# Transposing DMAs singly behind k loads, expert weights behind the last y store, last logits from 16-bit parts

## The chip, the cores and the metric

The kernel runs on one core of a Trainium2 chip. Its engines work in parallel, each through its own queue of instructions: TensorE (PE, with the loading of weights shown as PEld), VectorE (DVE), ScalarE (ACT), GpSimd (POOL) and SyncE (SP), which here does little but issue DMAs, one after the other in the order of its queue. An engine that waits for a semaphore holds everything behind it in its queue. The metric is the device time of one execution in microseconds, the median of several runs.

## The reference

Three stages, each fed by the one before, all in float32:

```python
scores = scale * np.matmul(q, k.transpose(0, 1, 3, 2))       # 4 x 8 heads x 576 x 64
scores = np.where(mask, scores + bias[None], -1000000000.0)  # window of 128, ALiBi
attn = softmax(scores);  x = np.matmul(attn, v)              # -> (2304, 512)

h = x @ w_in                                                 # 512 -> 2048
g = np.maximum(h, 0.0) + alpha * np.minimum(h, 0.0)
y = g @ w_out                                                # 2048 -> 512

logits = y @ w_gate                                          # 512 -> 8
order = np.argsort(-logits.flatten())                        # greedy: best logits first,
...                                                          # one expert a token, 288 tokens an expert
out[mask] = np.maximum(y[mask] @ w1[e], 0.0) @ w2[e]         # for each of 8 experts
```

## The kernel before, in words

Up to about 551 us, attention and the MLP are interleaved. The MLP goes in 9 units `u` of 256 tokens (`NU = 9`), each in 16 slices `f` of 128 hidden columns (`FT = 16`); one slice of one unit is a slot, 144 in all. Attention is done in blocks of 128 tokens and halves of 4 heads, some slots ahead of the unit that needs it. What is done in which slot is written in a table: `at(slot, fn, args)` puts a step at a slot, and the loop goes through the slots. A scheduler with a simulated timeline then sets the order on each engine; within one engine it may put a step earlier or later than the table has it, and `tc.issue_after(instruction)` keeps what is issued in its block behind the named instruction.

For a slice, `l1` (L697) makes the first layer: 12 matmuls of 128x256 into the bank `ph` (products of two fp16 parts each). ACT scales it to `g` (L703), DVE takes the leaky maximum (L704), ACT rounds to fp16 `gh` (L722) and DVE takes the rest `gl` (L723). `l2` (L740) makes the second layer: 6 matmuls of 128x512 into `py`. In the last unit those of the last 11 slices (`ND = 11`) aren't done at once but kept in the list `rest`, to fill PE during the first search of the routing; `gh` and `gl` then lie in tiles `gs`.

The logits of the last unit don't wait for its y. `og` (L854, slots 125.5 to 128.5) multiplies a transposed copy of w_out with w_gate into the combined weights `WG` (float32), and `last_logits` (L670) adds, for every slice, two float32 matmuls of `g` with `WG` into `PL`, from which `last_y` makes the logits. The transposed copies, `wt`, are made by `og_load`: 8 transposing DMAs (L846) for each of 4 groups, all 8 at one place of the table, the groups at slots 60, 68, 76, 84 (`OG0 = 60`, `OGS = 8`). They are issued from SP's queue, as are the loads of q (L386), k (L406), v (L412) and the stores of y (L768). A v load needs the one buffer `vr`, whose last reader is DVE's L498; its first reader is L451.

Behind the last unit comes the routing, expert by expert: a search for the threshold, in five passes (PE matmuls and DVE operations, with `fill` taking second-layer matmuls from `rest` between them), then `index`, then `gather` (L1215: POOL's indirect DMAs read the expert's rows of y back from `y_dram`). In the first round `last_rows` scales the last two blocks of y on ACT (L1208) and stores them (L1209). `warm` (L1036) are matmuls without use that fill PE. `expert_weights` loads 512 KB for each of 8 slices of an expert (L1226, three buffers `wr`), ACT rounds them (L1231) and POOL or DVE takes the rest (L1234). `expert_x` transposes the gathered rows (L1267), `expert_1` (L1283), `expert_2` (L1301) and `expert_y` make the expert's output, which POOL scatters to `out`.

Of the kernel before, what the change touches and what calls it, by code (L numbers as in the profile page):

```python
# [8 lines left out]
F32 = mybir.dt.float32  # L9
F32R = mybir.dt.float32r  # L10
F16 = mybir.dt.float16
BF16 = mybir.dt.bfloat16
# [4 lines left out]
ALU = mybir.AluOpType  # L17
AX = mybir.AxisListType

LABEL = None  # L20
P = 128
H = 8
# [4 lines left out]
LEAST = 896 * 16  # L27
KG = 15
FW = 20
ND, OG0, OGS, OG1 = 11, 60, 8, 125.5  # L30
FILL = (6, 4, 12, 5, 5, 5, 2, 11, 99)
FG_ = 1
WP, WX_ = 10, 3
# [71 lines left out]
def attention_moe_kernel(ctx, tc, qt, kt, vt, wm, alpha, wg, we, out, NB=18, dbg=None):  # L105
    nc = tc.nc
    NU = NB // 2
# [3 lines left out]
    FT = 16  # L111
# [13 lines left out]
    wh, wl = {}, {}  # L125
# [228 lines left out]
        return "plain"  # L354


    QR, QH, QL, KR, VP, E, SM, ET, S_, XN = ({} for _ in range(10))
    XF, XH, XL, MN, VG, VI, VC, XS = {}, {}, {}, {}, {}, {}, {}, {}
    XT_ = {}
# [42 lines left out]
    def load_k(n):  # L402
        b, hf = divmod(n, 2)
        KR[n] = att.tile([P, 4, P], F32, name="kr", bufs=KB)
        for i in range(2):
            nc.sync.dma_start(KR[n][i * 64:(i + 1) * 64], kt[b, hf])  # L406

    def load_v(n):
        b, hf = divmod(n, 2)
# [250 lines left out]


    GF, GH, GL, PY, PH, GS = {}, {}, {}, {}, [], {}
    PL, rest, LAST = [], [], {}

    def last_logits(f):
        g = GF.pop((NU - 1, f))
        if not f:
            PL.append(psum.tile([P, 2, H], F32, name="pl", tag="sA", bufs=1))
        for i in range(2):
            LAST["pl"] = nc.tensor.matmul(PL[0][:, i], g[:, i * P:(i + 1) * P], WG[:, f], start=f + i == 0, stop=f == FT - 1,  # L670
                             skip_group_check=True)

    def prefill():
        rest.sort(key=lambda e: e[:3])
# [51 lines left out]
    def l2(u, f):  # L726
        if f == 0:
            PY[u] = [psum.tile([P, 512], F32, name=f"py{i}", tag=f"py{i}") for i in range(2)]
        if u < EARLY_U:
            g = GF.pop((u, f))  # L730
            for i in range(2):
                nc.tensor.matmul(PY[u][i], g[:, i * P:(i + 1) * P], wf[f][:, 512:], start=f == 0, stop=f == FT - 1)  # L732
            return
        gh, g = GH.pop((u, f)), GL.pop((u, f))
        if u == NU - 1:
            last_logits(f)
        for i in range(2):
            for j, (a, w) in enumerate(((gh, wh), (gh, wl), (g, wh))):
                def one(i=i, j=j, a=a, w=w):
                    nc.tensor.matmul(PY[u][i], a[:, i * P:(i + 1) * P], w[f][:, 512:], start=f == 0 and j == 0,  # L740
                                     stop=f == FT - 1 and j == 2)
                if u < NU - 1 or f < FT - ND:
                    one()
                else:
                    rest.append((i, f, j, one))
        if u == NU - 1 and f == FT - 1:
            rest.sort(key=lambda e: e[:3])
            rest[:] = [e[3] for e in rest]
# [74 lines left out]
    def last_y():  # L823
        u = NU - 1
        fill(FILL[1])
        nc.vector.tensor_scalar(L[:, NB - 2:], PL[0], YI[:, u:u + 1], None, op0=ALU.mult)
        find_scale()
        R[0]["cmp"] = best_of(R[0], slice(NB - 2, NB))

# [2 lines left out]
    def thirds(dst, src, rest):  # L832

        nc.scalar.activation(dst[0], src, AF.Copy)
        nc.vector.tensor_sub(rest, src, dst[0])
        nc.scalar.activation(dst[1], rest, AF.Copy)
        nc.vector.tensor_sub(dst[2], rest, dst[1])

    WG = consts.tile([P, FT, H], F32, name="wog")
    WT = {}  # L840

    def og_load(j):
        WT[j] = wpool.tile([P, 4, 2, 4, P], F16, name="wt", tag=f"wd{4 + j}")
        for i in range(4):
            for k, w in enumerate((wh, wl)):
                nc.sync.dma_start_transpose(out=WT[j][:, i, k], in_=w[4 * j + i][:, 512:])  # L846

    def og(j):
        t = WT.pop(j)
        pl = psum.tile([P, 4, 3, H], F32, name="pl", tag="pav" if j % 2 else "sB", bufs=1)  # L850
        for i in range(4):
            for c in range(4):
                for k in range(2):
                    nc.tensor.matmul(pl[:, i], t[:, i, k, c], wg3[:, c], start=c + k == 0, stop=c + k == 4)  # L854
        nc.vector.tensor_reduce(WG[:, 4 * j:4 * j + 4], pl.rearrange("p f i e -> p f e i"), axis=AX.X, op=ALU.add)

    def gate_parts():
        r = mlp.tile([P, 4, H], F32, name="wgr", tag="yt", bufs=1)
# [45 lines left out]
    def at(s, fn, *a):  # L904
        ev.setdefault(math.floor(s), []).append((s, len(ev.get(math.floor(s), ())), fn, a))
# [57 lines left out]
        at(WC + f, w_split, f)  # L963
    at(WC - .5, w_scales)
    for j in range(4):
        at(OG0 + OGS * j, og_load, j)
        at(OG1 + j, og, j)

    def do(fn, *a):
# [234 lines left out]
    def last_rows():  # L1204
        for i in range(2):
            b, u = NB - 2 + i, NU - 1
            y = ex.tile([P, 512], F32, name="row", bufs=3)
            LAST["row"] = nc.scalar.activation(y, PY[u][i], AF.Copy, scale=YI[:, u:u + 1])  # L1208
            nc.sync.dma_start(y_dram[b * P:(b + 1) * P], y)  # L1209

    def gather(p):
        r = R[p]
# [7 lines left out]
    def expert_weights(p, f):  # L1220
# [2 lines left out]
            r["reg"] = nc.sync.value_load(r["ei"][0:1, 0:1], min_val=0, max_val=NE - 1)  # L1223
        s = (p % 2) * 8 + f
        w = ex.tile([P, 1024], F32, name="wr", bufs=3)
        nc.sync.dma_start(w, we[bass.ds(r["reg"], 1), f].rearrange("o p n -> (o p) n"))  # L1226
        w_slot(s)
        for i in range(2):
            h = slice(i * 512, (i + 1) * 512)
# [272 lines left out]
```

## Time and profile before

| what | before |
|---|---|
| median of 3 runs | 849.34 us (848.4 to 850.53) |
| profiled execution | 849.54 us |
| its span | 847.8 us |
| mean granted TensorE clock | 0.965 |
| PE busy | 801.5 us (95%) |
| PEld busy | 652.2 us (77%) |
| DVE busy | 577.8 us (68%) |
| ACT busy | 457.9 us (54%) |
| POOL busy | 278.9 us (33%) |
| first-layer matmuls (L697) | 1536, 199.3 us |

The busy times overlap, so they don't add up to the span. The span is what the profiler's records cover; the execution's own time is 1.7 us longer. Shares of the whole span say little on a kernel in stages; the rows further down are of single stretches. A name like L846 is a line of the kernel before.

### The profile page before, as it was taken

How to read it: one execution, taken by the hardware profiler on the slowest of the kernel's cores; microseconds unless marked ns; L12 is line 12 of the kernel's file. 1: busy time of each engine (PE TensorE's matmuls, PEld its weight loads, DVE VectorE, ACT ScalarE, POOL GpSimd, SP SyncE). 2: the span in 40 equal slices, each digit the busy share in tenths (PEclk: the TensorE clock that was granted, in tenths of full speed). 3: DMA queues.
4: the chain of work that ended last, by engine and by line, in shares of the span. 5: the costliest groups of instructions: out<-in, count | busy, mean ns of one | idle time of the engine just before them, and what ended most of it. 6: DMA issues, size and time to landing. Idle time of an engine off the chain costs nothing.

```text
span 847.8 us, 18203 instructions
## 1 busy us (share of the span) xinstructions
PE 801.5 (95%) x6854; PEld 652.2 (77%) x6854; DVE 577.8 (68%) x1748; ACT 457.9 (54%) x1097; POOL 278.9 (33%) x256
## 2 busy tenths in 40 slices
PE   7789999979999999999999999997999989999996
PEld 5667676757777767777777777856999879999995
DVE  6897688958687687887868753685677766752120
ACT  4899367746555565655655543413465444455531
POOL 4244020001110010101100000008799976888921
PEclk7699999999999999999999999997999999999998
DMA  8997101654021031121201000025466655556500
GB/s 298 278 350 235 33 26 50 119 106 138 26 84 51 30 98 41 47 80 51 81 33 38 2 2 26 2 99 152 148 199 194 197 163 170 156 175 198 165 29 29
DMA packets 49144, 93.22 MB, mean 110 GB/s; under 512 B 22800, under 2 KB 22816, under 8 KB 49056
## 3 DMA queue, kind: packets, MB, share of 16 engines
q1 hardware_dynamic: 45984, 82.62, 32.4%
q0 software_dynamic: 3072, 9.44, 3.5%
q8 instruction: 54, 0.88, 0.4%
q14 instruction: 34, 0.28, 0.1%
HBM read 78.40 MB, written 9.44 MB: 104 GB/s over the span
## 4 chain that ended last, share of the span: by engine, by line
PE 77%; DVE 9%; ACT 4%; DMA 3%; issue 3%; SPq 2%; POOL 2%; another core or an unknown queue 0%; POOLq 0%; ACTq 0%; DVEq 0%
PE ph L697 21%; PE py L740 17%; PE pyx L1301 12%; PE phx L1283 10%; PE S L533 3%; PE py L732 2%; SPq L846 2%; PE pav L627 2%; PE pav L619 2%; PE prt L1072 2%; PE pt L568 1%; DVE wf L182 1%; DMA vr<-in_v_dram 1%; DMA wr<-in_we_dram 1%; PE pt L648 1%
## 5 line engine op out<-in xcount | busy, mean ns | idle before, releaser
L697 PE MATMUL ph<-xh,wp 128*128 128x256 f16 x1536 | 199.3, 273 | 0.3 <-DVE g L704 0.3
L697 PEld LDWEIGHTS <-wp 128*128 128x128 f16 x1536 | 148.6, 99 | 42.3 <-issue 1.6
L1234 POOL TENSOR_TENSOR ws<-wr,ws 128x512 fp32r<-128x512 f32 x128 | 160.2, 1286 | 13.4 <-ACT ws L1231 12.4
L434 POOL TENSOR_TENSOR ks<-kr,ks 64x512 fp32r<-64x512 f32 x34 | 49.0, 1447 | 289.0 <-ACT ks L433 277.8
L740 PE MATMUL py<-wp,gh 128*128 128x512 f16 x468 | 131.3, 381 | 4.8 <-ACT gh L722 4.8
L703 ACT ACTIVATE g<-ph,sg 128x256 f32<-128x256 f32 x144 | 67.3, 468 | 101.5 <-PE ph L697 100.1
L1301 PE MATMUL pyx<-hh,ws 128*128 128x288 f32 x512 | 109.6, 300 | 0.0
L1231 ACT ACTIVATE ws<-wr 128x512 fp32r<-128x512 f32 x128 | 73.4, 627 | 50.6 <-DMA wr<-in_we_dram 35.8
L704 DVE SCALAR_TENSOR_TENSOR g<-ph,sa,g 128x256 f32<-128x256 f32 x144 | 69.1, 480 | 44.3 <-ACT g L703 44.0
L1283 PE MATMUL phx<-exh,ws 128*128 128x288 f32 x512 | 86.8, 307 | 0.2
L1301 PEld LDWEIGHTS pyx<-hh,ws 128*128 128x128 f32 x512 | 84.4, 188 | 0.0
L740 PE MATMUL py<-wp,gl 128*128 128x512 f16 x234 | 78.7, 382 | 0.6 <-DVE gl L723 0.6
L1283 PEld LDWEIGHTS phx<-exh,ws 128*128 128x128 f32 x512 | 74.9, 194 | 1.0 <-PE pox L1319 0.4
L1301 PE MATMUL pyx<-hl,ws 128*128 128x288 f32 x256 | 75.5, 295 | 0.0
L722 ACT ACTIVATE gh<-g 128x256 f16<-128x256 f32 x117 | 48.4, 413 | 49.3 <-DVE g L704 43.4
L740 PEld LDWEIGHTS <-gh 128*128 128x128 f16 x468 | 44.0, 98 | 36.1 <-ACT gh L722 5.4
L723 DVE TENSOR_TENSOR gl<-g,gh 128x256 f16<-128x256 f32 x117 | 53.1, 454 | 16.1 <-ACT gh L722 15.9
L1290 DVE SCALAR_TENSOR_TENSOR hl<-phx,hh 128x288 fp32r<-128x288 f32 x64 | 28.7, 454 | 51.7 <-ACT hh L1289 50.8
L559 ACT ACTIVATE e<-e,mn 128x128 f32<-128x128 f32 x116 | 45.1, 391 | 10.6 <-DVE mn L556 10.4
L1289 ACT ACTIVATE hh<-phx 128x288 fp32r<-128x288 f32 x64 | 25.4, 405 | 43.6 <-PE phx L1283 31.4
L1301 PEld LDWEIGHTS pyx<-hl,ws 128*128 128x128 f32 x256 | 48.2, 188 | 0.0
L1283 PE MATMUL phx<-exl,ws 128*128 128x288 f32 x256 | 46.9, 307 | 0.0
(291 smaller groups left out, 1549.9 us busy)
## 6 DMA issues: line engine op xcount, KB each, us to landing
wr<-in_we_dram SPq DMA_DIRECT2D x64, 512.0 KB
raw<-in_wm_dram SPq DMA_DIRECT2D x16, 1023.8 KB
kr<-in_k_dram SPq DMA_DIRECT2D x68, 128.0 KB
qr<-in_q_dram SPq DMA_DIRECT2D x64, 128.0 KB
y_dram<-y SPq DMA_DIRECT2D x16, 256.0 KB
vr<-in_v_dram SPq DMA_DIRECT2D x13, 256.0 KB
whole<-in_v_dram SPq DMA_DIRECT2D x4, 256.0 KB
whole<-in_q_dram SPq DMA_DIRECT2D x4, 128.0 KB
```

The costliest lines, as they stand in the source:

```text
L434: nc.gpsimd.tensor_sub(ks[64:], KR[n][64:], f32(ks[64:]))
L559: nc.scalar.activation(e[:, h], e[:, h], AF.Exp, bias=mn[:, h:h + 1], scale=-1.0, accum_out=SM[b][:, hh:hh + 1])
L697: LAST["l1"] = nc.tensor.matmul(ph, w[f][:, c * P:(c + 1) * P], x[u][:, c, :], start=i == 0, stop=i == 4 * len(pairs) - 1)
L703: KEPT[order.index((u, f))] = nc.scalar.activation(g, ph, AF.Copy, scale=sg)
L704: TURN[order.index((u, f))] = nc.vector.scalar_tensor_tensor(g, ph, sa, g, op0=ALU.mult, op1=ALU.max)
L722: nc.scalar.activation(gh, g, AF.Copy)
L723: nc.vector.tensor_sub(gl, g, gh)
L740: nc.tensor.matmul(PY[u][i], a[:, i * P:(i + 1) * P], w[f][:, 512:], start=f == 0 and j == 0, stop=f == FT - 1 and j == 2)
L1231: nc.scalar.activation(wh[s][:, h], w[:, h], AF.Copy)
L1234: (nc.vector if on_dve else nc.gpsimd).tensor_sub(wl[s][:, h], w[:, h], f32(wh[s][:, h]))
L1283: nc.tensor.matmul(ph, w[s][:, c * P:(c + 1) * P], x[:, c], start=i == 0, stop=i == 11)
L1301: nc.tensor.matmul(py, w[s][:, cs], r[x][f], start=i == 0, stop=i == 23)
```

## The change

Three parts. The first: the 32 transposing DMAs of w_out stand singly in the table, every second slot from 48 on (48, 50, ... 110), each kept behind the k load that was issued last. The second: of expert 0's weight loads only the first (`WE = 1`) may go ahead of the store of the last y rows; the others are kept behind it. The third: the last unit's logits of slices 0 to 14 are made of the parts `gh` and `gl` and of `WG` split in three bf16 parts (`WG3`; `gh` with three of them, 24 columns, `gl` with two, 16 columns), into four columns of partial sums that one DVE reduction adds; slice 15 stays in float32. The split of `WG` is 4 small operations for each of 4 groups, two on ACT and two on DVE.

```diff
-ND, OG0, OGS, OG1 = 11, 60, 8, 125.5
+ND, OG0, OGS, OG1 = 11, 48, 2, 125.5
+WE = 1
...
-            nc.sync.dma_start(KR[n][i * 64:(i + 1) * 64], kt[b, hf])
+            LAST["ld"] = nc.sync.dma_start(KR[n][i * 64:(i + 1) * 64], kt[b, hf])
...
     def last_logits(f):
         g = GF.pop((NU - 1, f))
         if not f:
-            PL.append(psum.tile([P, 2, H], F32, name="pl", tag="sA", bufs=1))
+            PL.append(psum.tile([P, 2, 4, H], F32, name="pl", tag="sA", bufs=1))
         for i in range(2):
-            LAST["pl"] = nc.tensor.matmul(PL[0][:, i], g[:, i * P:(i + 1) * P], WG[:, f], start=f + i == 0, stop=f == FT - 1,
-                             skip_group_check=True)
+            s = slice(i * P, (i + 1) * P)
+            if f == FT - 1:
+                LAST["pl"] = nc.tensor.matmul(PL[0][:, i, 3], g[:, s], WG[:, f], start=False, stop=True,
+                                              skip_group_check=True)
+                continue
+            for j, (a, k) in enumerate(((GH, 3), (GL, 2))):
+                nc.tensor.matmul(PL[0][:, i, :k], a[NU - 1, f][:, s], WG3[:, f, :k], start=f + i + j == 0,
+                                 stop=f == FT - 2, skip_group_check=True)
...
-        nc.vector.tensor_scalar(L[:, NB - 2:], PL[0], YI[:, u:u + 1], None, op0=ALU.mult)
+        new = L[:, NB - 2:]
+        nc.vector.tensor_reduce(new, PL[0].rearrange("p b i e -> p b e i"), axis=AX.X, op=ALU.add)
+        nc.vector.tensor_scalar(new, new, YI[:, u:u + 1], None, op0=ALU.mult)
...
-    def og_load(j):
-        WT[j] = wpool.tile([P, 4, 2, 4, P], F16, name="wt", tag=f"wd{4 + j}")
-        for i in range(4):
-            for k, w in enumerate((wh, wl)):
-                nc.sync.dma_start_transpose(out=WT[j][:, i, k], in_=w[4 * j + i][:, 512:])
+    def og_load(m):
+        j, i, k = m // 8, m % 8 // 2, m % 2
+        if m % 8 == 0:
+            WT[j] = wpool.tile([P, 4, 2, 4, P], F16, name="wt", tag=f"wd{4 + j}")
+        with tc.issue_after(LAST["ld"].ins):
+            nc.sync.dma_start_transpose(out=WT[j][:, i, k], in_=(wh, wl)[k][4 * j + i][:, 512:])
...
-        nc.vector.tensor_reduce(WG[:, 4 * j:4 * j + 4], pl.rearrange("p f i e -> p f e i"), axis=AX.X, op=ALU.add)
+        wj = WG[:, 4 * j:4 * j + 4]
+        nc.vector.tensor_reduce(wj, pl.rearrange("p f i e -> p f e i"), axis=AX.X, op=ALU.add)
+        r = mlp.tile([P, 4, H], F32, name="wgr", tag="yt", bufs=1)
+        thirds([WG3[:, 4 * j:4 * j + 4, i] for i in range(3)], wj, r)
...
-        at(OG0 + OGS * j, og_load, j)
+        for m in range(8 * j, 8 * j + 8):
+            at(OG0 + OGS * m, og_load, m)
...
-            nc.sync.dma_start(y_dram[b * P:(b + 1) * P], y)
+            LAST["store"] = nc.sync.dma_start(y_dram[b * P:(b + 1) * P], y)
...
-        nc.sync.dma_start(w, we[bass.ds(r["reg"], 1), f].rearrange("o p n -> (o p) n"))
+        with nullcontext() if p or f < WE else tc.issue_after(LAST["store"].ins):
+            nc.sync.dma_start(w, we[bass.ds(r["reg"], 1), f].rearrange("o p n -> (o p) n"))
```

In what follows, `wp_...` are the fp16 parts of the MLP's weights, `vr`, `kr`, `qr` the buffers of v, k and q. First SP's queue, in the middle of the interleaved stage. Before:

```order
L846 DMA_TRANSPOSE wt<-wp_1250 128x4x128 x4
L406 DMA kr<-in_k_dram 64x512 x2
L386 DMA qr<-in_q_dram 64x512 x2
L846 DMA_TRANSPOSE wt<-wp_1367 128x4x128 x4
L846 DMA_TRANSPOSE wt<-wp_1474 128x4x128 x4
L846 DMA_TRANSPOSE wt<-wp_1580 128x4x128 x4
L412 DMA vr<-in_v_dram 128x512
L846 DMA_TRANSPOSE wt<-wp_1695 128x4x128 x4
```

SP's queue now, from the place of the first transposes:

```order
L408 DMA kr<-in_k_dram 64x512 x2
L858 DMA_TRANSPOSE wt<-wp_1097 128x4x128 x2
L388 DMA qr<-in_q_dram 64x512 x2
L408 DMA kr<-in_k_dram 64x512 x2
L858 DMA_TRANSPOSE wt<-wp_1097 128x4x128 x2
L408 DMA kr<-in_k_dram 64x512 x2
L858 DMA_TRANSPOSE wt<-wp_1172 128x4x128 x2
L414 DMA vr<-in_v_dram 128x512
```

The transposes stood in blocks, twelve of them in a row ahead of one v load; they stand in ones and twos, behind k loads, and eleven of the 32 directly ahead of a v load (five times two, once one). The first stands several k, q and v loads later than before.

PE in the last unit, at the end of one slice's first layer and the start of the next's. Before (`wog` is `WG`):

```order
L697 LDWEIGHTS wp_1474
L697 MATMUL ph<-xh,wp_1474 128x256
L670 MATMUL pl<-wog,g 128x8 x2
L697 LDWEIGHTS wp_1580
L697 MATMUL ph<-xh,wp_1580 128x256
```

PE at such a place now (`wog_164` is `WG3`, `gs` holds `gh` and `gl`):

```order
L705 LDWEIGHTS wp_1581
L705 MATMUL ph<-xh,wp_1581 128x256
L678 LDWEIGHTS gs
L678 MATMUL pl<-wog_164,gs 128x24
L678 LDWEIGHTS gs
L678 MATMUL pl<-wog_164,gs 128x16
L678 LDWEIGHTS gs
L678 MATMUL pl<-wog_164,gs 128x24
L678 LDWEIGHTS gs
L678 MATMUL pl<-wog_164,gs 128x16
L705 LDWEIGHTS wp_1581
```

One float32 group of two became four 16-bit matmuls with their weight loads; they work on the slice two slots back.

SP's queue around the two stores of the last y rows (L1209 before, L1225 now). Before:

```order
L768 DMA y_dram<-y 128x512 x4
L1209 DMA y_dram<-row 128x512
L1223 TENSOR_LOAD ei
L1223 ISA x2
L1226 ISA
L1226 DMA wr<-in_we_dram 128x1024
L1226 ISA
L1226 DMA wr<-in_we_dram 128x1024
L1226 ISA
L1226 DMA wr<-in_we_dram 128x1024
L1209 DMA y_dram<-row 128x512
```

The same place now:

```order
L776 DMA y_dram<-y 128x512 x4
L1225 DMA y_dram<-row 128x512
L1239 TENSOR_LOAD ei
L1239 ISA x2
L1243 ISA
L1243 DMA wr<-in_we_dram 128x1024
L1225 DMA y_dram<-row 128x512
L1243 ISA
L1243 DMA wr<-in_we_dram 128x1024
```

Three loads of expert weights stood ahead of the second store; now it is one.

## Rows read from the trace of the kernel before

**Rows 1.** Page, chain of work that ended last: shares of the span by engine

```profile
PE 77%; DVE 9%; ACT 4%; DMA 3%; issue 3%; SPq 2%; POOL 2%; another core or an unknown queue 0%; POOLq 0%; ACTq 0%; DVEq 0%
```

**Rows 2.** Windows: us, busy (count) of PE PEld DVE ACT POOL, PEclk, DMA share, GB/s

```profile
180.00:200.00 20.00, 15.53 (x118) 11.40 (x116) 11.84 (x39) 9.81 (x28) 2.54 (x2) 0.83 0.58 145
200.00:548.00 348.00, 344.27 (x3160) 258.42 (x3159) 258.24 (x762) 190.56 (x509) 27.97 (x22) 1.00 0.15 46
```

**Rows 3.** Timeline of SP's queue: start us, us, queue, line, operation, out<-in, count

```profile
167.41 16.62 SPq L846 DMA_TRANSPOSE wt<-wp  x12
184.13 0.53 SPq L412 DMA_DIRECT2D vr<-in_v_dram  x1
```

**Rows 4.** Timeline of DVE and PE, 177 to 191 us: [idle before <-releaser]

```profile
177.64 0.75 DVE L498 SCALAR_TENSOR_TENSOR v<-vr,vc,v 128x512 f16<-128x512 f32 x1 [0.79 <-ACT v L493]
...
187.09 0.69 DVE L451 TENSOR_REDUCE vc<-vr 128x1 f32<-128x512 f32 x1 [6.25 <-DMA vr<-in_v_dram]
...
188.67 1.89 PE L740 MATMUL py<-wp,gh 128*128 128x512 f16 x4 [4.47 <-ACT gh L722]
```

**Rows 5.** Windows of 1 us, columns as in rows 2 (PEclk third from the right)

```profile
187.00:188.00 1.00, 0.00 (x0) 0.00 (x0) 0.91 (x2) 0.00 (x0) 0.00 (x0) 0.71 0.73 142
...
194.00:195.00 1.00, 1.00 (x10) 0.91 (x9) 0.98 (x3) 0.00 (x0) 0.00 (x0) 0.88 0.88 332
```

**Rows 6.** Chain that ended last, in order of time: start us, us, what

```profile
184.13 2.94 DMA vr<-in_v_dram
...
238.92 2.78 DMA vr<-in_v_dram
```

**Rows 7.** Waits of DVE and of SP's queue, whole span: us in sum, count, longest

```profile
DVE vc L451 <- DMA vr<-in_v_dram: 14.2, 9, 6.3
...
SPq L412 <- DVE v L498: 26.1, 4, 15.9
```

**Rows 8.** Chain that ended last, one slice of the last unit

```profile
538.48 0.35 PE pl L670 x4
538.82 1.32 PE ph L697 x12
```

**Rows 9.** Timeline of PE: the matmuls on transposed w_out

```profile
513.32 0.95 PE L854 MATMUL pl<-wg,wt 128*128 128x24 bf16 x32
```

**Rows 10.** Timeline of DVE and ACT in the last unit

```profile
529.61 0.18 DVE L877 TENSOR_REDUCE L<-pl 128x8 f32<-128x24 f32 x1 [1.44 <-PE pl L876]
...
548.61 0.47 ACT L703 ACTIVATE g<-ph,sg 128x256 f32<-128x256 f32 x1 [0.23 <-PE ph L697]
...
549.64 0.42 ACT L722 ACTIVATE gs<-g 128x256 f16<-128x256 f32 x1 [0.55 <-DVE g L704]
```

**Rows 11.** Timeline of SP's queue, 556 to 570 us

```profile
559.02 0.32 SPq L1209 DMA_DIRECT2D y_dram<-row  x1
565.56 1.43 SPq L1226 DMA_DIRECT2D wr<-in_we_dram  x3
568.65 0.34 SPq L1209 DMA_DIRECT2D y_dram<-row  x1
```

**Rows 12.** Timeline of ACT, POOL and PE, 572 to 583 us

```profile
572.74 1.15 ACT L1231 ACTIVATE ws<-wr 128x512 fp32r<-128x512 f32 x2 [0.58 <-DMA wr<-in_we_dram]
...
574.33 1.13 POOL L1215 DMA_INDIRECT xg<-y_dram,ix  x1 [19.81 <-DVE rs L1061]
...
581.71 0.90 PE L1267 MATMUL ptx<-ident,xg 96*128 96x96 f32 x4 [1.18 <-DMA xg<-y_dram,ix]
```

**Rows 13.** Windows around the stores and the gather, columns as in rows 2

```profile
560.50:561.00 0.50, 0.50 (x16) 0.28 (x12) 0.47 (x4) 0.00 (x0) 0.00 (x0) 1.00 0.08 25
...
572.00:573.00 1.00, 1.00 (x11) 0.90 (x10) 0.90 (x3) 0.42 (x2) 0.00 (x0) 1.00 0.11 43
...
586.00:587.00 1.00, 1.00 (x22) 1.00 (x22) 0.41 (x3) 0.81 (x2) 1.00 (x2) 0.61 0.84 98
```

**Rows 14.** Waits of ACT, expert phase: us in sum, count, longest

```profile
ACT hh L1289 <- remote: 3.9, 1, 3.9
```

More of the change, by code (lines that the diff above doesn't have):

```diff
@@ L354, in kind_of @@
         return "plain"
+    LAST = {}
     QR, QH, QL, KR, VP, E, SM, ET, S_, XN = ({} for _ in range(10))
@@ L662, in attention_moe_kernel @@
     GF, GH, GL, PY, PH, GS = {}, {}, {}, {}, [], {}
-    PL, rest, LAST = [], [], {}
+    PL, rest = [], []
     def last_logits(f):
@@ L733, in l2 @@
             return
-        gh, g = GH.pop((u, f)), GL.pop((u, f))
         if u == NU - 1:
             last_logits(f)
+        gh, g = GH.pop((u, f)), GL.pop((u, f))
         for i in range(2):
@@ L839, in attention_moe_kernel @@
     WG = consts.tile([P, FT, H], F32, name="wog")
+    WG3 = consts.tile([P, FT, 3, H], BF16, name="wog3")
     WT = {}
-    def og_load(j):
-        WT[j] = wpool.tile([P, 4, 2, 4, P], F16, name="wt", tag=f"wd{4 + j}")
-        for i in range(4):
-            for k, w in enumerate((wh, wl)):
-                nc.sync.dma_start_transpose(out=WT[j][:, i, k], in_=w[4 * j + i][:, 512:])
+    def og_load(m):
[4 more added lines that the diff above has]
+            nc.sync.dma_start_transpose(out=WT[j][:, i, k], in_=(wh, wl)[k][4 * j + i][:, 512:])
     def og(j):
```

## The prediction

> **What bounds the kernel now.** I began with the chain of work that ended last, summed by engine: TensorE (PE) holds 77% of it, SP's queue only 2% and DMA 3% [rows 1]. So time can be won only where PE stops, or does work that can be done in less; and a stop is to be judged in its own stretch. The table by stretch says where that is: from 200 to 548 us PE is busy 344.27 of 348 us at a granted clock of 1.00, but from 180 to 200 only 15.53 of 20, at a mean clock of 0.83 [rows 2]. The rest of the reading is of three places.
>
> The first place is that stretch. SP works through twelve transposing DMAs from 167.41 on, 16.62 us long, 1.39 each, and only then, at 184.13, issues the load of the next v block [rows 3]. Its buffer was free at 178.39: that is when VectorE's (DVE) last read of the old block ends, 177.64 + 0.75 [rows 4]. The load lands 2.94 us after its issue [rows 6], DVE starts on it at 187.09 after waiting 6.25 us, and PE, which needs what DVE makes of it, resumes at 188.67 after 4.47 us of idleness [rows 4]. The granted clock falls in 187 to 188 (mean 0.71: the fall from 2.4 to 1.2 GHz lies at 187.4) and is back in 194 to 195 (mean 0.88: at 194.24) [rows 5]. So PE was idle to 188.67 and then ran 5.57 us at the half clock.
>
> The second is the last unit of tokens, where PE alternates between twelve matmuls of the first layer, 1.32 us, and one float32 group of logits, 0.35 us [rows 8].
>
> The third is the end of the search, where GpSimd (POOL) gathers the rows of expert 0 at 574.33. SP issues three loads of expert weights from 565.56 and the store of the last y rows only at 568.65 [rows 11].
>
> **The transposes, spread (A).** Nothing is computed less: 32 of them stay, and their data moves at a DMA share of 0.15 [rows 2], so it is a matter of SP's queue alone. Removed: the block of twelve ahead of the v load. It would be issued at about 178.5 and land at 181.4, 5.7 us sooner. PE's work after it, 188.67 before, could begin at 183.0; but PE had other work until 188.67 − 4.47 = 184.20, so all of the 4.47 goes, and no more. With the gap goes, if the gap is what the clock fell on, the stretch at half clock: 5.57 us in which half of the work is done, so 2.8 us. What is late next there is DVE: it is busy 11.84 of the 20 us [rows 2], and without the wait of 6.25 the same work has 13.75 us, which leaves it 86% full; PE may be held by it in small pieces.
>
> Added: in the new order a transpose or two stands directly ahead of six of the later v loads, eleven in all, and others behind k loads, ahead of q loads and y stores. A v load that is ready goes at most 2 × 1.39 us later. SP has slack for it: in four waits, 26.1 us in sum, it stands idle for a v buffer [rows 7], and time spent on a transpose before the buffer is free costs nothing. On the other side, DVE waited for v data nine times, 14.2 us in sum, 6.3 of it the case above [rows 7]; the other eight share 7.9, so v data comes just in time. I find one load with no slack and take half a transpose for it, 0.7; from 0 to 1.39 for the one, and the rival below for all. The queue behind, q, k and y, has whole slots of slack. A = 4.47 + 2.8 − 0.7 = 6.6; bounds 7.3 (no cost) and 3.8 (the clock falls all the same).
>
> **The logits in parts (C).** For each of the first fifteen slices a group of 0.35 us [rows 8] is replaced by four small matmuls on 16-bit parts, 24 and 16 columns wide. The nearest row is the kernel's own 128x24 bf16 matmul on transposed weights: 32 of them in 0.95 us, 0.030 each, and so 0.12 us for four [rows 9]. PE saves 0.23 a slice. In the first five slices, where second-layer matmuls fill in, that is 5 × 0.23 = 1.15. In the next ten ScalarE (ACT) comes in: its g starts at 548.61, it waits 0.55 for DVE, and its gh ends at 549.64 + 0.42 = 550.06, 1.45 us in all [rows 10]; PE would need 1.32 + 0.12 = 1.44, before 1.67. With a little for the hand-over a slice goes from 1.67 to 1.46: 10 × 0.21 = 2.1. Against it stands one reduction more on DVE in the tail, 0.18 by its like [rows 10], on the way to the search: 0.2. The sixteen small operations that split the gate weights, eight on DVE at 0.18 each, 1.4 us, lie in a region where DVE is busy 258.24 of 348 us [rows 2]; I put them at nothing, and at 1.4 if that cover is gone. C = 1.15 + 2.1 − 0.2 = 3.1. The upper bound is 15 × 0.23 − 0.2 = 3.3. The lower one is below nothing: if each small matmul with its weight load costs what one of the twelve does, 1.32 / 12 = 0.11, then a slice takes 0.44, 0.09 more than now, and C = −15 × 0.09 − 0.2 = −1.6. I take the upper side because the 32 differ from these only in a few columns.
>
> The row shows 30 ns for a small matmul with its weight load. The Trainium skill, "TensorE: Matmul & The Clock Gate", section "Back-to-back issue gap", gives about 81 ns for a sustained pair of weight load and matmul of 128 columns; by that figure a slice would cost 0.32, C would be 0.2 and the time 840.8. The trace disagrees for narrow ones, by [rows 9].
>
> **The store ahead of two loads (B).** Before, the second store of y rows goes out behind three loads of 512 KB and its data lies in the queues with theirs: the DMA engines fall to a share of 0.11 only in 572 to 573 [rows 13]. POOL's gather starts at 574.33, 2.2 us after the data's end at about 572.1, though the profile names a DVE operation as what ended the wait [rows 12]. The first store, alone in its queue, was issued at 559.02 and in 560.5 to 561 the engines are all but empty, a share of 0.08 [rows 11, 13]: so 1.6 us. With one load only ahead, the second store is done at about 568.65 + 1.6 = 570.25 and the gather can start at 572.4: 1.9 us sooner. What then moves along: POOL's weight differences, and PE's first transposes of gathered rows, which wait for the gather [rows 12]. The two loads behind the store go 3.4 us later and land near 574; their last ACT conversion, at 572.74 before [rows 12], would end near 575.5, well ahead of PE's first use at 582, so it is hidden; without that cover it would cost what they are late, 1.6. B = 1.9. Below, nothing (another releaser). Above, more than its own 1.9: the clock is half until 586.8 (mean 0.61 in 586 to 587 [rows 13]), though PE works without a break from 581.71 [rows 12]. 5.07 us at half are 2.5; if the shorter wait keeps the clock up, B = 4.4. I take 1.9, since the wait for the gathered rows is shortened, not removed.
>
> **Sum**, against the profiled execution's 849.54 (its span of 847.8 and 1.7 around it, which I take to stay): 6.6 + 3.1 + 1.9 = 11.6, so 837.9. The median of the runs is 0.2 lower, which I leave out.
>
> **Rivals.**
>
> 1. *Slower: the spread transposes hold v loads.* Place: the six v loads with transposes directly ahead. Price: if each of the eleven passes its 1.39 us on to PE, 15.3, and A is 7.3 − 15.3 = −8.0; the time is 852.5. It decides from 12.3 / 11 = 1.1 us a transpose on, where all three gains are eaten. For it: v data is just in time. Against it: the v load behind the block landed 2.94 us after its issue, one behind none 2.78 [rows 6], so the transposes' data doesn't slow a load, and SP idles ahead of most of them. Chance 0.07, of which 0.03 that half is passed on and the time is within the 0.3% (2.5 us) that a measurement of this kernel can tell from no change.
> 2. *Small matmuls at 0.11.* C = −1.6, the time 842.6. For it: they stand between streams with other weights and come in pairs of different inputs; against it [rows 9]. Chance 0.10.
> 3. *The gather doesn't move.* DVE, not the store, releases it, as the profile says [rows 12]; B = 0, 839.8. Against it: by that row the releaser was done long before. The Trainium skill, "DMA: Bandwidth & Descriptors", section "Anatomy of one DMA — SWDGE (gpsimd) path", says that most of a fixed 2 us goes to the receipt of the last write, HBM's the heaviest; by it the store would be the releaser, and the trace agrees with its 2.2 us from the data's end to the gather. Chance 0.10.
> 4. *More is won: the clock stays up at the gather.* B = 4.4, 835.4. ACT has one wait of 3.9 us in the expert phase, released from outside its records [rows 14]; ACT's queue gets eight instructions more ahead of that, and if that wait goes or moves, as much again may change, either way; down to 833.5 or so. Chance 0.20.
> 5. *DVE takes SP's place in 180 to 200.* The idle time is cut into small ones and the clock falls as before: A = 3.8, 840.7. For it: DVE 86% full. Chance 0.09.
>
> **How the numbers follow.** The forecast has 0.44, the rivals 0.56. The range goes from 833.5 (rival 4) to 844.5, where rivals 2 and 3 meet: 6.6 − 1.6 = 5.0. It leaves out rival 1, 0.07, and about 0.1 for rivals that come together. Faster by over 0.3%: the forecast and rivals 2 to 5, 0.93; within: 0.03; slower: 0.04.
>
> **What would show it.** In the changed kernel's trace: A, no idle of PE over 1 us in 180 to 200, the clock at 1.00 there, v loads issued within a transpose of their buffer's release; wrong if DVE's waits for v data sum to more than 14.2. C, a slice of the last unit in 1.46 us, the four small matmuls in 0.12; wrong if the slice stays at 1.67 or over. B, POOL's first gather 3.8 us after the second store's issue, not 5.7; wrong if the gather starts as long as before after the end of the search. It would all be wrong if the order of the steps between 200 and 510 moved so that PE loses more than a few tenths per hundred us there.

## The result, and the profile after

| | before | changed |
|---|---|---|
| median | 848.75 us (six runs, 848.4 to 850.53) | 837.81 us (six runs, 835.8 to 841.03) |
| ratio, with its 95% interval | | 0.9875 [0.9851, 0.9898] |
| profiled execution, its span | 849.54, 847.8 us | 840.6, 838.9 us |
| mean granted clock | 0.965 | 0.969 |

The forecast was 837.9 us, 11.6 less than the profiled execution of before; the medians differ by 10.9, and 0.8 of the difference is where the forecast was counted from: that execution took 849.54 us, the median of before is 848.75. The profiled execution of the changed kernel is one of its slower ones, 8.9 us below that of before, and the terms below are read from these two traces first.

A convenient measure is the lead: by how much the same instruction starts sooner in the changed kernel. First the rows of before that front it (the timelines of PE and POOL: start, length, engine, line, operation, [idle before <-releaser]):

```profile
301.69 0.20 PE L627 MATMUL pav<-vp,et 128*128 128x64 f16 x1 [1.90 <-DVE et L606]
...
547.04 1.47 PE L697 MATMUL ph<-xh,wp 128*128 128x256 f16 x12
...
554.06 0.60 PE L1072 MATMUL prt<-ob,cmp 128*128 128x8 f16 x18
...
582.63 1.52 PE L1283 MATMUL phx<-exh,ws 128*128 128x288 f32 x4
...
839.68 0.91 POOL L1330 DMA_INDIRECT out_dram<-row,ix  x1 [21.93 <-DVE row L1325]
```

The same instructions in the changed kernel, and those that answer to [rows 9] (508.78) and [rows 12] (563.38):

```profile
295.44 0.20 PE L629 MATMUL pav<-vp,et 128*128 128x64 f16 x1 [1.90 <-DVE et L608]
...
508.78 0.95 PE L866 MATMUL pl<-wg,wt 128*128 128x24 bf16 x32
...
538.48 1.47 PE L705 MATMUL ph<-xh,wp 128*128 128x256 f16 x12
...
545.67 0.61 PE L1088 MATMUL prt<-ob,cmp 128*128 128x8 f16 x18
...
563.38 1.14 POOL L1231 DMA_INDIRECT xg<-y_dram,ix  x1 [17.25 <-DVE w L799]
...
570.17 1.51 PE L1300 MATMUL phx<-exh,ws 128*128 128x288 f32 x4
...
830.73 0.92 POOL L1347 DMA_INDIRECT out_dram<-row,ix  x1 [21.92 <-DVE row L1342]
```

The lead is 6.25 us at 300 us of before's time, 4.54 at 513, 8.56 at the last slice of the first layer, 8.39 at the first search, 10.95 at the first gather, 12.46 at the first expert matmul, and 8.95 at the end. So each part brought something, 1.7 us were lost between 300 and 513, and 3.5 in the expert phase.

**The transposes.** In SP's queue the v load now goes out at 178.61, not behind twelve transposes at 184.13 [rows 3]; later ones stand singly or in pairs:

```profile
178.61 0.34 SPq L414 DMA_DIRECT2D vr<-in_v_dram  x1
...
202.74 2.62 SPq L858 DMA_TRANSPOSE wt<-wp  x2
...
312.14 1.60 SPq L858 DMA_TRANSPOSE wt<-wp  x1
313.84 0.52 SPq L414 DMA_DIRECT2D vr<-in_v_dram  x1
```

DVE, which waited 6.25 us [rows 4], reads the block without waiting, and PE's longest stop there is 0.33 (timelines of DVE and PE):

```profile
181.18 0.69 DVE L453 TENSOR_REDUCE vc<-vr 128x1 f32<-128x512 f32 x1
...
186.85 0.39 PE L535 MATMUL S<-ks,ql 128*128 128x256 f32 x1 [0.33 <-DVE ql L422]
```

By the table of stretches (columns as in [rows 2]) PE is busy 19.57 of 20 us there at a clock of 1.00, not 15.53 at 0.83; the waits of DVE for v data fell from 14.2 us [rows 7] to 9.1:

```profile
180.00:200.00 20.00, 19.57 (x182) 15.17 (x181) 18.12 (x60) 13.84 (x38) 3.83 (x3) 1.00 0.31 89
```

```profile
DVE vc L453 <- DMA vr<-in_v_dram: 9.1, 8, 1.6
```

**The logits.** PE's timeline in the last unit: by starts, four small matmuls take 0.10 us (532.73 to 532.83; the printed length of a group goes past the start of the next) and a slice 1.41 (532.73 to 534.14), where [rows 8] had 0.35 and 1.67:

```profile
532.73 0.25 PE L678 MATMUL pl<-wog,gs 128*128 128x24 bf16 x4
532.83 1.47 PE L705 MATMUL ph<-xh,wp 128*128 128x256 f16 x12
534.14 0.25 PE L678 MATMUL pl<-wog,gs 128*128 128x24 bf16 x4
```

ACT's timeline shows why the chain that I took for a limit is none: an operation printed with 0.42 us is followed by the next after 0.38 (534.02 to 534.40) or 0.32 (535.53 to 535.85), so printed lengths can't be added. And g starts 0.10 us behind the printed end of PE's group (532.83 + 1.47 = 534.30, g at 534.40), as it did before (547.04 + 1.47 = 548.51, g at 548.61 [rows 10]): it is still PE that sets the pace of 1.41:

```profile
534.02 0.42 ACT L730 ACTIVATE gs<-g 128x256 f16<-128x256 f32 x1 [0.56 <-DVE g L712]
534.40 0.47 ACT L711 ACTIVATE g<-ph,sg 128x256 f32<-128x256 f32 x1
535.53 0.42 ACT L730 ACTIVATE gs<-g 128x256 f16<-128x256 f32 x1 [0.65 <-DVE g L712]
535.85 0.46 ACT L711 ACTIVATE g<-ph,sg 128x256 f32<-128x256 f32 x1
```

**The store.** SP's queue around the second row store, and the profile's list of DMA issues from 556 to 582 us (its last number is the time from issue to landing):

```profile
557.16 0.36 SPq L1243 DMA_DIRECT2D wr<-in_we_dram  x1
560.25 0.32 SPq L1225 DMA_DIRECT2D y_dram<-row  x1
560.76 14.06 SPq L1243 DMA_DIRECT2D wr<-in_we_dram  x5
```

```profile
y_dram<-row SPq DMA_DIRECT2D x1, 256.0 KB, 2.2
```

The store lands 2.2 us after its issue, at about 562.4, and the gather's row starts 0.9 to 1.0 later, at 563.38: 3.13 us behind the store's issue, where it was 5.68 [rows 11, 12].

**What was lost.** Between 300 and 513 it is one place. In both kernels PE stops there for 1.90 us (301.69 and 295.44 in the rows above). Behind the stop, the clock of before stays up and that of the changed kernel is half for 3.4 us. Before, in stretches of 1 us:

```profile
302.00:303.00 1.00, 1.00 (x24) 0.93 (x21) 1.00 (x3) 0.00 (x0) 0.00 (x0) 1.00 0.07 16
303.00:304.00 1.00, 1.00 (x8) 0.59 (x6) 0.57 (x2) 0.00 (x0) 0.00 (x0) 1.00 0.03 4
```

After:

```profile
296.00:297.00 1.00, 1.00 (x17) 0.88 (x15) 1.00 (x3) 0.00 (x0) 0.00 (x0) 0.50 0.40 50
297.00:298.00 1.00, 1.00 (x7) 0.69 (x6) 0.31 (x1) 0.00 (x0) 0.00 (x0) 0.50 0.29 57
```

In the expert phase this execution has a stop of 1.54 us at 652, where ACT waited for expert weights (1.79 us for the load), with half clock behind it; the large stop of before (3.54 us at 692 to 696) is there in both, 3.45 at 683 to 687 (PE's timelines, after and then before):

```profile
653.54 0.41 PE L1088 MATMUL prt<-ob,cmp 128*128 128x8 f16 x10 [1.54 <-DVE cmp L912]
...
686.87 0.41 PE L1088 MATMUL prt<-ob,cmp 128*128 128x8 f16 x10 [3.45 <-DVE cmp L912]
```

```profile
695.74 0.41 PE L1072 MATMUL prt<-ob,cmp 128*128 128x8 f16 x10 [3.54 <-DVE cmp L897]
```

### The profile page after: what moved, and what is told of

The parts are those of the page before. It is cut to its first block, busy times and chain, and to the rows that moved or that the text cites. A ratio compares the mean times of both kernels' runs of the same rounds, so it can differ in the third digit from the quotient of the medians.

```text
span 838.9 us, 18221 instructions
## 1 busy us (share of the span) xinstructions
PE 796.7 (95%) x6854; PEld 647.0 (77%) x6854; DVE 578.8 (69%) x1757; ACT 458.0 (55%) x1105; POOL 281.5 (34%) x256
## 4 chain that ended last, share of the span: by engine, by line
PE 80%; DVE 7%; DMA 5%; ACT 2%; issue 2%; POOL 1%; SPq 1%; another core or an unknown queue 0%; POOLq 0%; DVEq 0%; ACTq 0%
PE ph L705 22%; PE py L748 18%; PE pyx L1318 12%; PE phx L1300 11%; PE S L535 3%; PE py L740 2%; PE prt L1088 2%; PE pav L629 2%; DMA raw<-in_wm_dram 2%; PE pav L621 1%; PE pt L570 1%; DMA wr<-in_we_dram 1%; DVE wf L184 1%; PE pty L879 1%; PE pt L650 1%
## 5 line engine op out<-in xcount | busy, mean ns | idle before, releaser
L436 POOL TENSOR_TENSOR ks<-kr,ks 64x512 fp32r<-64x512 f32 x34 | 51.2, 1511 | 282.3 <-ACT ks L435 271.0
```

The source lines that it names most:

```text
L436: nc.gpsimd.tensor_sub(ks[64:], KR[n][64:], f32(ks[64:]))
```

## The experiments

Each ratio is to runs of the kernel before on the same chip. Chips differ: the kernel before had a median of 842.4 and 843.7 us on two of them and of 848.8 to 850.6 on the three others. So beside the ratio each verdict rests on the lead at places of the trace. The table gives what the lead gained or lost in five stretches (by the starts of the same matmuls; the last two are bounded by the last first-layer matmul and the expert's first second-layer matmul):

| kernel | v load, 193 us | stop at 300 | to 513 | last unit, 513 to 548 | search to expert 0, 548 to 600 |
|---|---|---|---|---|---|
| changed | 6.54 | -1.64 | -0.08 | 4.03 | 3.37 |
| again (1) | 6.55 | -1.65 | -0.57 | 4.02 | 3.08 |
| again (2) | 6.54 | -1.67 | -0.15 | 4.03 | 3.69 |
| transposes alone | 6.53 | -1.68 | -0.61 | -0.02 | -0.30 |
| logits alone | -0.36 | 0.00 | 0.00 | 4.02 | 0.52 |
| store alone | -0.39 | -1.55 | 0.01 | 0.00 | 2.92 |
| singly, not held | -0.13 | -1.56 | 0.00 | 0.00 | 0.14 |
| blocks behind v loads | 6.54 | 0.00 | 0.02 | 0.00 | -0.14 |

Between the first two columns the transposes alone and the blocks behind v loads gained 1.2 and 1.1 us more at one place, near 249 us, and no other kernel did. What differs there is one DVE operation on the attention weights, beside a POOL operation on k: in twelve profiles it takes 1.16 to 1.47 us, and PE stops for about 1 us behind it; in these two it started within 0.04 us of POOL's, took 0.42, and PE doesn't stop (DVE's timelines, before and then blocks behind v loads):

```profile
244.59 1.42 DVE L606 TENSOR_TENSOR et<-et 128x512 f16<-128x512 f16 x1
```

```profile
240.06 0.42 DVE L607 TENSOR_TENSOR et<-et 128x512 f16<-128x512 f16 x1
```

It is the meeting of the same two operations as in the section on the stop at 300, so this gain belongs to the moment at which they met, not to what the edits were meant to do.

### The three parts, each alone

```diff
-ND, OG0, OGS, OG1 = 11, 60, 8, 125.5
+ND, OG0, OGS, OG1 = 11, 48, 2, 125.5
...
+        with tc.issue_after(LAST["ld"].ins):
+            nc.sync.dma_start_transpose(out=WT[j][:, i, k], in_=(wh, wl)[k][4 * j + i][:, 512:])
```

> The first part alone: the 32 transposing DMAs stand singly behind k loads, the rest is the kernel before. Theory (SP's block of twelve held one v load): PE's 4.47 us of idleness at 184 to 189 and 2.8 us of the stretch at half clock go, 0 to 0.7 come back by transposes ahead of v loads: 6.5 us less than the kernel before (848.8), so 842.3. Rival 1 (transposes hold the later v loads, 1.1 us or more each): 848 or over. Rival 5 (DVE keeps PE waiting and the clock falls all the same): 3.8 us less, 845.0. The three parts add up if a_only, b_only and c_only together give the 10.9 us of the whole change.

Measured: 837.25 us, ratio 0.9925 [0.9896, 0.9954] to 842.39, 6.3 us less by the ratio (5.1 by the medians). The lead at the v load is the forecast's, 6.53. One of the transposes does hold a v load: DVE waits 2.10 us for the data there, against 0.83 where the transposes stand behind the load (the run with blocks, below), PE stops 0.42 us, and 0.59 of the lead is gone (timelines of DVE and PE):

```profile
314.77 0.69 DVE L452 TENSOR_REDUCE vc<-vr 128x1 f32<-128x512 f32 x1 [2.10 <-DMA vr<-in_v_dram]
...
315.90 1.47 PE L698 MATMUL ph<-xh,wp 128*128 128x256 f16 x12 [0.42 <-DVE g L705]
```

The other ten cost nothing that the trace shows. So rival 1 falls, with its mechanism real in one place of six, and rival 5 falls too.

```diff
+            for j, (a, k) in enumerate(((GH, 3), (GL, 2))):
+                nc.tensor.matmul(PL[0][:, i, :k], a[NU - 1, f][:, s], WG3[:, f, :k], start=f + i + j == 0,
+                                 stop=f == FT - 2, skip_group_check=True)
```

> The third part alone: the last unit's logits from 16-bit parts; transposes and stores as before. Theory after the trace of the changed kernel (a slice goes from 1.67 to 1.41 us and isn't held by ACT): 15 x 0.26 - 0.2 = 3.7 us less, 845.1. The prediction's term (ACT's chain holds ten slices at 1.46): 3.1 less, 845.7. Rival 2 (0.11 us for each small matmul): 1.6 us more, 850.4.

Measured: 837.18 us, ratio 0.9937 [0.9909, 0.9964], 5.3 us less by the ratio. By the trace the last unit gains 4.02 us and the tail gives 0.17 back, so 3.85: rival 2 falls.

```diff
+        with nullcontext() if p or f < WE else tc.issue_after(LAST["store"].ins):
```

> The second part alone: expert 0's weight loads but the first stand behind the store of the last y rows. Theory: POOL's first gather starts 3.8 us after the second store's issue (5.7 before), 1.9 us sooner, 846.9. Rival 4 (and the clock stays up there or is back sooner): 4.4 less, 844.4. Rival 3 (the gather is released by DVE's index, not by the store): 848.8, and the gather stays 5.7 us behind the store's issue.

Measured: 839.25 us, ratio 0.9957 [0.9931, 0.9984], 3.6 us less by the ratio (3.1 by the medians). The gather comes 3.12 us behind the store (SP's and POOL's timelines), so rival 3 falls and the term was too small:

```profile
568.40 0.32 SPq L1210 DMA_DIRECT2D y_dram<-row  x1
...
571.52 1.13 POOL L1216 DMA_INDIRECT xg<-y_dram,ix  x1 [17.25 <-DVE w L792]
```

That the store is what releases the gather is shown by the six profiles in which its landing is kept: the gather's row starts 0.9 to 1.0 us behind the landing in all of them, whether the store lands 2.1 to 2.2 us after its issue, as with one load ahead, or 4.6 and 4.9, as with three (logits alone and transposes alone; the line is of the latter, where the store is issued at 562.25 and the gather starts at 568.11):

```profile
y_dram<-row SPq DMA_DIRECT2D x1, 256.0 KB, 4.9
```

The three ratios make 15 us, the whole change on that chip 9.5 (13.5 and 9.1 by the medians), with intervals of some 2.5 us on each of the singles and of 3.4 on the whole: by the times alone it isn't shown that the parts add up. The traces are less loose: from 150 us to the expert's first second-layer matmul the singles gained 5.1, 4.3 and 1.1 us, 10.5 in sum, and the whole 11.3. These sums hold chance as well: the half clock at 300 stands in two of the singles and once in the whole, and the gain near 249 in the first single alone. Place by place the parts add up: 6.53 at the v load, 4.02 in the last unit and -0.30 + 0.52 + 2.92 = 3.14 behind it, against 6.55, 4.02 and 3.08 in the whole.

### The whole change again, twice

> The whole change once more, for a second profile. In the first one (840.6 us, 2.8 over the median) PE stood 1.9 us at 293 and 1.5 us at 652 with a stretch at half clock behind each. Theory (what differs between executions of this kernel is where the granted clock falls behind such a short stop): the median stays at 837.8, the stop at 293 is there again, as it is in the kernel before at 300, but the clock behind it needn't fall; an execution without those two stretches takes 836 to 838. Rival (the change's order makes the stop at 652 each time): the stop at 652 with ACT waiting for expert weights stands in this profile too.

Measured: 833.26 us, ratio 0.9887 [0.9847, 0.9927]. The stop at 293 is there, with half clock behind it; the one at 652 is not (in the next one a shorter stop stands there, 0.74 us, with 3.4 us of half clock, and 0.6 to 0.7 us in two of the edited versions below, so it isn't excluded that the change has a part in it). Nor is the large one at 683, and this has nothing to do with the change: the profiles of the three parts alone, on the same chip, lack it as well. On the chips of the other runs ACT has, in this stretch, one wait of 2.8 to 3.9 us released from outside its records (in one profile its end is put down to a DVE operation), as in [rows 14]; on the two fast chips there is none in any of five profiles. With the half clock behind it that is most of the 6 to 8 us between chips: 5.8 us of the lead of this profile arise between 685 and 705. What releases it the traces don't tell.

> The whole change a third time, beside the two next kernels on one chip. Theory: 10 to 12 us less than the kernel before (ratio 0.986 to 0.989); 0.6 us lost near 318 by the one transpose ahead of a v load, and PE at half clock for 6.8 us behind the first gather.

Measured: 837.62 us, ratio 0.9854 [0.9812, 0.9895] to 850.6. Two details missed: no 0.6 us were lost near 318 (0.13), and behind the first gather the clock was half for 3.4 us, not 6.8.

### What about the transposes does it

Singly in the table, but without the hold:

```diff
+ND, OG0, OGS, OG1 = 11, 48, 2, 125.5
...
+        with nullcontext():
+            nc.sync.dma_start_transpose(out=WT[j][:, i, k], in_=(wh, wl)[k][4 * j + i][:, 512:])
```

> The transposes alone again, singly in the table at every second slot from 48 on, but not held behind k loads. Theory (the hold is the change, since SP's queue, issuing what is ready, otherwise still gets twelve of them in a row ahead of the v load): PE's stop at 184 to 189 stays at 3.7 to 4.5 us, with half clock behind it, and the time is that of the kernel before. Rival (finer steps in the table suffice): the stop is gone and the time 6 us less.

Measured: 851.14 us, ratio 1.0023 [0.9998, 1.0047]. SP's queue has the block as before, twelve ahead of the v load:

```profile
166.73 16.41 SPq L848 DMA_TRANSPOSE wt<-wp  x12
183.24 0.53 SPq L413 DMA_DIRECT2D vr<-in_v_dram  x1
```

and PE stops 3.46 us. Finer steps in the table did nothing; the hold did it.

In the old blocks of eight, each held behind a v load:

```diff
+            LAST["v"] = nc.sync.dma_start(VP[b, "raw"], vt[b])
...
+                with tc.issue_after(LAST["v"].ins) if j in (0, 1, 2, 3) and "v" in LAST else nullcontext():
+                    nc.sync.dma_start_transpose(out=WT[j][:, i, k], in_=w[4 * j + i][:, 512:])
```

> The kernel before with the transposes in their four blocks of eight (11 us of SP's queue each) but each block held behind a v load; the first of them come later for it. Theory (only the v load held up PE): the stop at 184 to 189 is gone as with the first part, 6.5 us sooner at that place, and blocks of 11 us ahead of q and k loads cost nothing or under 1 us each, since these have slots of slack. Rival (q and k loads have no more slack than v loads): new stops of several us behind each block, 8 to 15 us in sum, and the time is that of the kernel before or over.

Measured: 844.64 us, ratio 0.9946 [0.9928, 0.9965], 4.6 us less. The lead at the v load is the same 6.54, and behind the blocks of 10.4 to 11.3 us nothing is lost (0.02 us from 300 to 513):

```profile
286.19 0.34 SPq L413 DMA_DIRECT2D vr<-in_v_dram  x1
286.62 10.48 SPq L848 DMA_TRANSPOSE wt<-wp  x8
297.21 3.08 SPq L387 DMA_DIRECT2D qr<-in_q_dram  x4
```

So only that v load had no slack; q and k loads stood 11 us of it.

### How many loads may go ahead of the store

```diff
-WE = 1
+WE = 2
```

> The whole change, but two of expert 0's weight loads may go ahead of the last y store (one in the change, three before). Theory (the gather waits for the later of the store's landing and DVE's index; a load of 512 KB ahead delays the landing by 1.5 us, and with one load ahead the index is the later one): the gather starts 4.2 us behind the store's issue, between 3.1 (one load) and 5.7 (three). Rival (the gather is released by the index alone, and the gain is of another kind): 3.1 us, as with one.

Measured (a single run of 838.8 us): the gather comes 3.31 us behind the store's issue, near one load's 3.13, not halfway to three loads' 5.68:

```profile
561.36 0.33 SPq L1225 DMA_DIRECT2D y_dram<-row  x1
...
564.67 1.13 POOL L1231 DMA_INDIRECT xg<-y_dram,ix  x1 [17.44 <-DVE rs L800]
```

1.5 us a load was wrong: the second costs 0.2, the third 2.4. That the store's place among the loads sets the gather's start is shown by the three. Why the step is so uneven no run tests, but the landings fit it: in the profile of the transposes alone the three loads land 0.8, 2.0 and 4.3 us behind the store's issue, and the store 0.6 us behind the last of them. A store takes 2.2 us anyway, so the second load is in by then, and only the third holds the store up.

### Versions meant to be faster

Transposes singly in the table and held behind v loads, and matmuls without use in PE's short stops around the first gather:

```diff
+            warm(12)
...
-                warm(WX_ if k < 2 else 0)
+                warm((4, 8, 0)[k])
...
-        with tc.issue_after(LAST["ld"].ins):
+        with tc.issue_after(LAST["v"].ins):
```

> The whole change with two further edits: the transposes are held behind v loads instead of k loads (so none stands ahead of a v load), and matmuls without use fill three short stops of PE around the first gather (12 ahead of the index matmuls, 4 and 8 instead of 3 and 3 between the transposes of gathered rows). Theory: the 0.6 us that a transpose ahead of a v load cost near 316 goes, and the stretch at half clock behind the gather (6.8 us, from 569) goes or is shorter, up to 2.5 us: 2 to 3 us less than the whole change, so 11 to 14 less than the kernel before. Rival (the clock falls there whatever PE does): 0.6 less.

Measured: 837.16 us, ratio 0.9861 [0.9837, 0.9886]. No half clock behind the gather, as hoped; but the lead fell by 0.6 and 1.3 at the first slices of two later units, and PE waited 1.88 us for DVE in the search (1.93 in the third profile of the change). The transposes stood in fours behind v loads, 5.1 to 5.3 us; that they cost the lead isn't shown. At the second of the two places it is again a DVE operation beside POOL's operation on k (453.80, 1.26 us), with a stop of PE of 0.95 behind it (DVE's timeline):

```profile
453.89 1.46 DVE L608 TENSOR_TENSOR et<-et 128x512 f16<-128x512 f16 x1
```

No gain over the change.

The useless matmuls alone, on the whole change:

> The whole change, and matmuls without use in three short stops of PE around the first gather (12 ahead of the index matmuls, 4 and 8 instead of 3 and 3 between the transposes of gathered rows). Theory (the granted clock falls there because PE stops several times in ten us): the clock stays at 1.00 there and the expert's first matmul group ends 0.7 us sooner than without, so 0 to 1 us less than the whole change in the time. Rival (they only delay the work behind them): the clock falls all the same, 0 to 1 us more.

Measured: 835.97 us, ratio 0.9817 [0.9781, 0.9854]; beside it the whole change 0.9854. The clock was half for 3.4 us, in both, and the last stretch of the table gained 3.79 against 3.69. The medians' 1.65 us are within the intervals; the theory isn't borne out.

The same with the transposes in blocks of eight behind v loads:

> As the one with useless matmuls, but the transposes stay in blocks of eight, each held behind a v load. Theory (blocks of eight behind a v load cost nothing, as in the run with that edit alone, and no transpose stands ahead of a v load): no loss near 318, 0.6 us less than with single transposes behind k loads, and up to 1.7 less where the clock does not fall at 293; ratio to the kernel before 0.983 to 0.987. Rival (8 transposes of 11 us hold up q and k loads when the rest has become faster): not below the whole change.

Measured: 836.27 us, ratio 0.9821 [0.9786, 0.9856]. No loss near 318 and none at the stop of 300, as expected (0.00 and 0.00); 1 us less was gained around the gather. Not told apart from the whole change.

### The stop at 300

```diff
-        nc.gpsimd.tensor_sub(ks[64:], KR[n][64:], f32(ks[64:]))
+        (nc.vector if n in (24,) else nc.gpsimd).tensor_sub(ks[64:], KR[n][64:], f32(ks[64:]))
```

> The whole change, and one subtraction of k's low part (64x512, the one at 293.83 that runs on POOL beside DVE's last operation on the attention weights et) made on DVE behind that operation instead. Every profile so far has PE stopped for 1.90 us there, where DVE's operation took 1.41 us, until 0.28 us after POOL's had ended; alone its like take 0.41. Theory (DVE's operation waits for POOL's): it takes 0.41 again and PE's stop is 0.9 us; if the granted clock then stays up, the slices behind it lose nothing, 2.6 us less than the whole change at 300 us. Rival (the operation is long for another reason): 1.41 again, PE's stop 1.9 us.

In the changed kernel (timelines of DVE and POOL) the two overlap:

```profile
293.97 1.41 DVE L608 TENSOR_TENSOR et<-et 128x512 f16<-128x512 f16 x1
...
293.83 1.26 POOL L436 TENSOR_TENSOR ks<-kr,ks 64x512 fp32r<-64x512 f32 x1 [3.92 <-ACT ks L435]
```

With POOL's operation moved, DVE's takes 0.41 and PE's stop is 0.90 (timelines of DVE and PE), and the clock stays at 1.00:

```profile
294.63 0.41 DVE L608 TENSOR_TENSOR et<-et 128x512 f16<-128x512 f16 x1
...
295.10 0.20 PE L629 MATMUL pav<-vp,et 128*128 128x64 f16 x1 [0.90 <-DVE et L608]
```

```profile
297.00:298.00 1.00, 1.00 (x9) 0.61 (x7) 0.82 (x2) 0.00 (x0) 0.00 (x0) 1.00 0.10 9
```

The theory holds: the lead gains 0.95 at the stop instead of losing 1.65. About 1 of these 2.6 us went again: the order of the work behind it changed, and 1.5 us were lost until 513, against 0.1 to 0.8 without. 828.5 us, ratio 0.9826 [0.9796, 0.9856]; not told apart from the change's three ratios of 0.9875, 0.9887 and 0.9854. It is the lowest time of all, but on one of the two faster chips.

## Why the prediction was right, point by point

- **Transposes, 6.6 forecast.** By its steps 4.47 of idleness and 2.8 of half clock, 7.3, and 0.7 for one held load. Measured 6.54 for the first two at that place in every profile in which the v load stands ahead of the block (6.53 to 6.55), and 0.1 to 0.8 for the held load (0.09 to 0.78 in the six profiles with the order of the change). "All of the 4.47 goes" was a little too much: 0.33 is left, and DVE is what is late next, as named. That only this v load was without slack is shown by the blocks of eight.
- **Logits, 3.1 forecast.** 3.85: PE saves 0.26 a slice and not 0.23 (0.10 for four, not 0.12), and ACT's chain doesn't hold the ten slices at 1.46. The step that was mis-sized is "1.45 us in all": printed lengths of ACT's operations were added, though the next one starts 0.04 to 0.10 us before each ends, and PE, not ACT, sets the pace. The Trainium skill, "TensorE: Matmul & The Clock Gate", section "Back-to-back issue gap", has 81 ns a pair for 128 columns, by which, as an estimate, four would take 0.32. The trace has 0.10 for four of 24 and 16 columns; the figure isn't for such narrow ones.
- **Store, 1.9 forecast.** 2.6 us at the gather, 2.9 at the expert's second layer with the store alone, 3.1 to 3.7 with everything. The store's landing after 2.2 us, and the gather 0.9 to 1.0 later, replace "1.6 + 2.2": the mechanism is right, the two lengths were too long by 0.7. The upper bound, the clock staying up, was 4.4; the clock fell for 6.8 or 3.4 us instead of 10.2, so some of it came. That the store did this isn't shown: with the logits alone, the gather as late as before, it was 6.8 as well.
- **Not in the sum.** The half clock behind the unchanged stop at 300, 1.65, and the expert phase, where this one execution lost 3.0. The first is in each of the seven profiles that keep the transposes out of blocks (all but the one with POOL's operation moved), in two of the four that keep them where they were, and in neither of the two with blocks behind v loads; what tips it stays open.

So the mechanisms were right (but for the ACT chain), yet that the total came out within 0.1 us of the median is luck: two terms that were 0.7 and 1.0 to 1.8 too small met a loss of 1.7 that I hadn't seen, and the forecast was counted from an execution 0.8 us over the median. Of the rivals, 1, 2, 3 and 5 fell; 4 came halfway, but ACT's wait of [rows 14] neither went nor moved with the change: it goes with the chip.

## What to carry to other kernels

A queue that issues in order should be read for what stands ahead of the one transfer that has no slack: here one load of many, and it hardly mattered whether the transposes went singly or in eights, only that they no longer stood ahead of that load. A step moved in a table moves nothing if a scheduler sets the order; the hold does, so the order is to be read, not the table. And a term for "what limits next" is to be built from starts of successive operations, not from printed lengths.

## What the hardware showed that I had not expected

- A DVE operation on fp16 with two inputs that takes 0.41 us took 1.41 beside a POOL operation on k, and ended 0.28 us after it; moving POOL's operation gave 0.41. Where the two started within 0.04 us of each other, near 240, DVE's took 0.42 and POOL's 1.5 to 1.6 us instead of 1.26. The Trainium skill, "SBUF — State Buffer", section "SBUF: two separate sides", has it that the two share a pair of ports which one of them holds for its whole instruction while the other is blocked; the trace agrees.
- The same stop of PE, 1.90 us with the same work around it, is followed by full clock in some executions and by 3.4 us of half clock in others, 1.65 us either way. A forecast for such a place in this kernel can't be sharper than that.
- The same program takes 842 to 844 us on two chips and 849 to 851 on three, most of it one wait in the expert phase and the half clock behind it. Times of two kernels from different chips can't be compared; leads by place within the trace can, up to that wait.
